# Scores of ten head pairs from float32r parts, sums of batch 0 by matmul, and an order made from other durations

## The chip, the cores and the metric

The kernel runs on one core of one Trainium2 chip. Its time is the device time of one execution in microseconds. It was executed three times; one further execution was profiled.

## What is computed

Softcapped attention over 4 batches, 12 heads, 448 positions and head size 64, then an MLP with squared ReLU; `cap` is 30.

```python
scores = scale * np.matmul(q, k.transpose(0, 1, 3, 2))
scores = cap * np.tanh(scores / cap)
scores = scores - np.max(scores, axis=-1, keepdims=True)
attn = np.exp(scores)
attn = attn / (np.sum(attn, axis=-1, keepdims=True) + 1e-09)
x = np.matmul(attn, v)              # heads side by side: 1792 x 768
h = x @ w_in                        # 768 x 2048
r = np.maximum(h, 0.0)
out = (r * r) @ w_out               # 2048 x 768
```

## The kernel before

Heads are taken in pairs, 24 of them, six to a batch, by `heads` (L187). A pair's scores come in four chunks of 112 keys. For a chunk, `qk` (L210) issues two float32 products of 64 rows, one for each head, in the two halves of the array, into a PSUM tile `s`; there are two such tiles. ScalarE (ACT) applies tanh (L224) and exp (L253). VectorE (DVE) adds the four chunks into `added` (L265). `pv` (L280) multiplies by `v` into `po`, with the heads side by side in columns. For the sums, `parts` (L346) transposes and reduces `added`, `whole_sum` (L353 to L360) makes reciprocals of it, `tr2` (L329) spreads them, `mult` (L334) scales, and `x_hi` and `x_lo` split the result in two float32r parts, `x`.

A branch at the start (L665) picks one of two programs by `cap`. With `cap` at most 40 the `bounded` one runs: no maximum is taken, and the sums go by DVE as said. The other has `ones` (L294), products with a tile of ones, and the steps `sums`, `tr1`, `rec` in the place of `parts` and `whole_sum`.

The weights come as 64-bit words that hold doubles. `convert` (L378) makes two float32r parts of each of 34 blocks, 16 of `w_in` and 18 of `w_out`, by `rebase` (L393, L395), `sign` and `low` (L405, L408), `whole` (L411), and the copies of L164/L166 and the differences of L169 into `w`. Batch 0 uses the blocks as they are converted; they are stored and loaded again for the other three batches. `unit` (L436) does the MLP: for each block and row tile three float32r products of 128 x 448, L455 to L457, into `f` (or `ff`); there are 2304 of them. ACT and DVE make `g` from it.

No loop over time stands in the code. Every piece of work is a `Step` with a key (a due time), a duration for each engine that may take it, and what it depends on. A planner at the end of `tile_body` (L544 to L638) takes the ready step of the lowest key for each engine, with these durations, buffer counts, and 0.15 us for PE when it goes over between whole products, products by rows (`qk`) and products by columns (`pv`). The order it finds is issued; each engine then runs its own list in order.

```python
            q = Step(T + (2 if b == 0 else QD) * c0, "PE", 0.75 * n_at, qk, [ready], new=s[cs] + t[cs], use=[raw], mode="rows")
```

Of the kernel before, what the change touches and what calls it, by code (L numbers as in the profile page):

```python
# [19 lines left out]
def tile_body(  # L20
# [11 lines left out]
    nc = tc.nc  # L32
# [10 lines left out]
    C0, LAT, TAIL = 4, 28, 30  # L43
    DMA, QSTEP, HOLD, PORT = 2.5, 2, 4, 15
    PVD, QD = 6, 2
    XH, GH, WH = 0.0, -2.0, 0.0
    ADD_FROM = 11
    PSTEP = [2, 2, 4, 4]
    W = [140, 145, 150, 120]
# [12 lines left out]
    def f(ap):  # L62
        return ap.bitcast(F32)
# [14 lines left out]
    for i in range(4):  # L78
        par = i % 2
        v32[par].append(const.tile([CP, NCH, 2 * D], F32, name=f"v32_{i}"))  # L80
        if not bounded:
            nc.vector.memset(v32[par][-1][:, :, D:2 * D] if par == 0 else v32[par][-1][:, :, 0:D], 1.0)
    nc.sync.dma_start(out=capb, in_=cap.to_broadcast([P, 1]))
    nc.vector.tensor_scalar_mul(capn, capb, -1.0)
    nc.vector.tensor_tensor(out=capa, in0=capb, in1=capn, op=ALU.max)
# [3 lines left out]
    if bounded:  # L89
        nc.scalar.activation(out=eps, in_=capa, func=AF.Exp, scale=-1.0)  # L90
        nc.vector.tensor_scalar_mul(eps, eps, 1e-9)
        added = [const.tile([P, 2, S], F32, name=f"added{i}") for i in range(2)]
        for a in added:
            nc.vector.memset(a[96:P], 0.0)
    else:
        nc.vector.memset(eps, 1e-9)

# [41 lines left out]
    steps = []  # L139

    class Step:
        def __init__(self, key, eng, dur, fn, deps=(), new=(), use=(), lag=0.15, behind=None, mode="full", port=False, calls=False):
            self.calls = calls
            self.key, self.fn, self.lag, self.mode = key, fn, lag, mode
            self.on, self.pen = dur if eng is None else ({eng: dur}, {eng: 0.0})
            self.any, self.taken, self.port = eng is None, False, port or eng is None
            self.new, self.use, self.after, self.wait = list(new), list(use) + list(new), [], 0
            for d in set(deps) | {u.maker for u in use}:
                d.after.append(self)
                self.wait += 1  # L150
# [19 lines left out]

    def COPY(n, act=0.0, dve=0.0):
        return (
            {"ACT": 0.1 + n * 0.00085, "DVE": 0.07 + n * 0.00055},
            {"ACT": act, "DVE": dve},
        )

    def EITHER(act, dve):
        return {"ACT": act, "DVE": dve}, {"ACT": 0.0, "DVE": 0.0}

    def SUB(n):  # L180
        return 0.07 + n * 0.00105
# [5 lines left out]
    def heads(p, T, n_at):  # L187
# [15 lines left out]

        ready = Step(T - 16, "SP", 1.5 * (p > 0), load, new=[raw], lag=3.0)
        got_v = Step(T, "SP", 1.4, load_v, new=vs, lag=3.0)

        tanhs = []
        for c0 in range(0, NCH, n_at):

            def qk(c0=c0):  # L210
                for c in range(c0, c0 + n_at):
                    ks = slice(c * CP, (c + 1) * CP)
                    for i in range(2):
                        r = slice(i * D, (i + 1) * D)
                        nc.tensor.matmul(  # L215
                            s[c].ap[0:CP, i, 0:S], raw.ap[r, 1, ks], raw.ap[r, 0], start=True, stop=True
                        )

            cs = slice(c0, c0 + n_at)
            q = Step(T + (2 if b == 0 else QD) * c0, "PE", 0.75 * n_at, qk, [ready], new=s[cs] + t[cs], use=[raw], mode="rows")  # L220
            for c in range(c0, c0 + n_at):

                def tanh(c=c):
                    nc.scalar.activation(out=t[c].ap, in_=s[c].ap[0:CP, :, 0:S], func=AF.Tanh, scale=c1[0:CP])  # L224

                tanhs.append(Step(T + 2 * c + 1, "ACT", 0.9, tanh, [q], use=[s[c], t[c]]))

        if not bounded:
            a = tanhs[0]
            for c in range(1, NCH):  # L230

                def top(c=c):
                    nc.vector.tensor_tensor(out=mx.ap, in0=t[0].ap if c == 1 else mx.ap, in1=t[c].ap, op=ALU.max)

                a = Step(
                    T + 2 * c + 3, "DVE", 1.01, top, [a, tanhs[c]], calls=c == NCH - 1,
                    new=[mx] * (c == 1), use=[t[c]] + ([t[0]] if c == 1 else [mx]), port=True,
                )
# [8 lines left out]
        for c in range(NCH):  # L247
# [6 lines left out]

            z = tanhs[c]
            if not bounded:
                z = Step(T + 14 + 2 * c, "DVE", 1.01, less, [a], use=[t[c], ma], port=True)
            exps.append(Step(T + EXP + 2 * c, "ACT", 0.95, exp, [z], use=[t[c]]))

        if n_add:  # L260
            ts = Buf("ts")
            for c in range(1, NCH):

                def add(c=c):
# [1 line left out]

                adds = [
                    Step(
                        T + EXP + 1 + 2 * c, "DVE", 1.01, add, exps[c - 1:c + 1] + adds,
                        new=[ts] * (c == 1), use=[t[c]] + ([t[0]] if c == 1 else [ts]), port=True,  # L270
                    )
                ]


        rows = [slice(0, D), slice(D, 2 * D)]

        by_ones = not bounded
# [16 lines left out]
        def ones(u, start, stop):  # L294
            for i in range(2):
                nc.tensor.matmul(
                    ss.ap[rows[i], 0:S], vs[i].ap[:, 0, rows[1 - i]], u.ap[:, i], start=start, stop=stop
                )

        n_pv = PSTEP[b]  # L300
# [50 lines left out]
        def whole_sum():  # L351
            r, o, z = (q.ap[:, i] for i in range(3))
            nc.vector.tensor_copy(o[0:64], r[64:128])  # L353
            nc.vector.tensor_tensor(out=z[0:64], in0=r[0:64], in1=o[0:64], op=ALU.add)
            nc.vector.tensor_copy(o[0:32], z[32:64])
            nc.vector.scalar_tensor_tensor(
                out=r[0:32], in0=z[0:32], scalar=eps[0:32], in1=o[0:32], op0=ALU.add, op1=ALU.add
            )
            for i in range(4):
                nc.vector.reciprocal(out=rc.ap[32 * i:32 * i + 32], in_=r[0:32, i // 2 * NB:(i // 2 + 1) * NB])  # L360

        T += NORM
        if by_ones:
            a = Step(T, None, EITHER(0.63, 0.56), sums, pvs[-1:], new=[sm], use=[ss])
            a = Step(T + 1, "DVE", 0.57, tr1, [a], new=[tr], use=[sm])
            a = Step(T + 1, "DVE", 0.17, rec, [a], new=[rc], use=[tr])
            a = Step(T + 1, "DVE", 0.56, tr2, [a], use=[rc, sm])
        else:
            a = Step(T, "DVE", 1.0, parts, adds, new=[q], use=[ts])
            a = Step(T, "DVE", 1.0, whole_sum, [a], new=[rc], use=[q])  # L370
            a = Step(T, "DVE", 0.64, tr2, [a], new=[sm], use=[rc])
        a = Step(T + 1, "DVE", 0.54, mult, [a] + pvs[-1:], new=[xf], use=[sm, po])
        a = Step(T + 2, None, COPY(448, dve=XH), x_hi, [a], new=[x], use=[xf])
        a = Step(T + 3, "DVE", SUB(448), x_lo, [a], use=[xf, x], port=True)
        x_t[b, h // 2], xdone[b, h // 2] = x, a
# [2 lines left out]
    def convert(T, src, dst, n):  # L378
# [44 lines left out]

        d = n / 6.0
        a = first = Step(T - 7, "SP", DMA * d, load, new=[raw], lag=4.0)
        m = Step(T, None, EITHER(0.91 * d, 0.83 * d), rebase, [a], new=[mag], use=[raw])
        a = Step(T, "DVE", 0.02 + 0.48 * d, sign, [a], new=[u], use=[raw], port=True)
        a = Step(T, "DVE", 0.02 + 0.48 * d, low, [a], use=[raw, u], port=True)
        a = Step(T, "DVE", 0.07 + 0.8 * d, whole, [a, m], use=[u, mag], port=True)
        a = Step(T, None, COPY(768 * d, dve=WH), w_hi, [a], new=[w], use=[u])  # L430
        a = Step(T, "DVE", SUB(768 * d), w_lo, [a], use=[u, w], port=True)
        loads[:] = [first]
# [32 lines left out]
    def up(T, d, b, m):  # L465
# [19 lines left out]
            sub(g.ap[:, 1], r.ap, f(g.ap)[:, 0])  # L485

        T += d
        a = Step(T, None, EITHER(0.54, 0.56), relu, done, new=[r], use=[hp])
        a = Step(T, "ACT", 0.53, square, [a], use=[r])
        a = Step(T, None, COPY(448, dve=GH), g_hi, [a], new=[g], use=[r])  # L490
        a = Step(T, "DVE", SUB(448), g_lo, [a], use=[r, g], port=True)
        g_t[b, m], gdone[b, m] = g, a
# [1 line left out]
    def down(T, d, b, dm, q, acc):  # L494
# [62 lines left out]
    while n_left:  # L557
        moved = False
        for e, q in ready.items():
# [15 lines left out]
            while q:  # L575
# [13 lines left out]
                if fit:  # L589
# [108 lines left out]
```

## Time and profile before

| what | value |
|---|---|
| median of 3 executions | 669.44 us (669.27 to 671.44) |
| profiled execution, its own time | 670.38 us |
| its span, first to last instruction | 668.6 us |
| PE busy | 646.4 us, 97% |
| DVE busy | 332.4 us, 50% |
| ACT busy | 333.5 us, 50% |
| granted clock of TensorE, mean | 0.989 |

The profiled execution took 1.8 us more than its span and 0.94 us more than the median. A busy PE is not a PE at its peak: matmuls are pipelined, and what one costs is the distance from its start to the next one's.

### The profile page before, as it was taken

Reading aid. Unit: us, or ns where it says so; the run is one execution under the profiler, and the core shown is the slowest. Engines: PE = TensorE matmul, PEld = TensorE weight load, DVE = VectorE, ACT = ScalarE, POOL = GpSimd, SP = SyncE. Lnnn points to the kernel's source line nnn. Section 1 sums busy time; section 2 is a strip of 40 time slices with the busy share of each in tenths; the row PEclk is TensorE's granted clock in tenths of the full one; section 3 lists DMA queues with packets and bytes.
Section 4 is the critical chain, followed back from the end, with each engine's and each line's share of the span. In section 5 each row is a group of like instructions: output and inputs, shape, how many; then the busy total and the mean of one; then the engine's idle time right before and its main releaser. Section 6 shows DMA issues by size and latency. Waiting matters only on the chain.

```text
span 668.6 us, 8034 instructions
## 1 busy us (share of the span) xinstructions
PE 646.4 (97%) x3072; PEld 486.2 (73%) x3072; DVE 332.4 (50%) x613; ACT 333.5 (50%) x456; POOL 0.2 (0%) x4
## 2 busy tenths in 40 slices
PE   4899998999999999999999999999999999999996
PEld 1234477667767798776798676767689999999996
DVE  3999999999999921565203146564620001110000
ACT  5899748677486425587202336858610005452000
POOL 0000000000000000000000000000000000000000
PEclk9799998999999999999999999999999999999999
DMA  8964587988899989864677576544348686666750
GB/s 204 301 181 131 154 264 269 331 283 273 297 311 333 336 286 335 236 181 137 191 239 235 182 235 184 166 156 140 97 156 262 223 280 227 222 187 205 257 162 31
DMA packets 57310, 148.46 MB, mean 222 GB/s; under 512 B 26288, under 2 KB 35504, under 8 KB 57264
## 3 DMA queue, kind: packets, MB, share of 16 engines
q1 hardware_dynamic: 57120, 147.64, 69.1%
q8 instruction: 26, 0.43, 0.3%
q10 hardware_dynamic: 144, 0.23, 0.1%
q14 instruction: 20, 0.16, 0.1%
HBM read 117.18 MB, written 30.67 MB: 221 GB/s over the span
## 4 chain that ended last, share of the span: by engine, by line
PE 88%; DVE 7%; DMA 2%; SPq 1%; issue 1%; ACT 1%; DVEq 0%
PE f L455 18%; PE f L457 17%; PE f L456 17%; PE s L215 10%; PE po L284 10%; PE ff L457 5%; PE ff L456 5%; PE ff L455 5%; DMA raw<-in_w_in_dram 2%; DVE added L265 1%; DVE u L411 1%; DVE w L169 1%; DVE rc L360 1%; DVE q L346 1%; DVE u L405 0%
## 5 line engine op out<-in xcount | busy, mean ns | idle before, releaser
L169 DVE TENSOR_TENSOR g<-r,g 128x448 fp32r<-128x448 f32 x64 | 39.6, 621 | 159.1 <-ACT g L164 158.9
L455 PE MATMUL f<-x,w 128*128 128x448 f32 x300 | 115.2, 384 | 3.0 <-DVE w L169 2.3
L457 PE MATMUL f<-x,w 128*128 128x448 f32 x300 | 110.5, 368 | 0.8 <-DVE x L169 0.7
L456 PE MATMUL f<-x,w 128*128 128x448 f32 x300 | 110.2, 367 | 0.0
L455 PE MATMUL f<-g,w 128*128 128x448 f32 x288 | 106.9, 371 | 0.5 <-DVE w L169 0.5
L457 PE MATMUL f<-g,w 128*128 128x448 f32 x288 | 105.2, 365 | 0.0
L456 PE MATMUL f<-g,w 128*128 128x448 f32 x288 | 105.2, 365 | 0.0
L224 ACT ACTIVATE t<-s,c 112x896 f32<-112x896 f32 x96 | 92.1, 1000 | 14.7 <-PE s L215 14.6
L253 ACT ACTIVATE t<-t,capa 112x896 f32<-112x896 f32 x96 | 96.3, 1039 | 0.2
L215 PE MATMUL s<-qkraw 64*112 64x448 f32 x368 | 83.6, 572 | 6.6 <-ACT t L224 6.6
L455 PEld LDWEIGHTS f<-x,w 128*128 128x128 f32 x300 | 56.7, 189 | 37.5 <-issue 24.4
L284 PE MATMUL po<-t,v 112*64 112x448 f32 x384 | 80.2, 561 | 0.0
L265 DVE TENSOR_TENSOR added<-added,t 112x896 f32<-112x896 f32 x48 | 52.1, 1085 | 48.7 <-ACT t L253 47.8
L455 PEld LDWEIGHTS f<-g,w 128*128 128x128 f32 x288 | 54.1, 188 | 14.5 <-issue 9.5
L457 PEld LDWEIGHTS f<-x,w 128*128 128x128 f32 x300 | 56.8, 189 | 6.4 <-DVE x L169 1.6
L505 ACT ACTIVATE o<-f 128x448 f32<-128x448 f32 x18 | 9.8, 545 | 102.8 <-PE f L457 102.8
L215 PEld LDWEIGHTS s<-qkraw 64*112 64x112 f32 x368 | 29.3, 174 | 43.2 <-issue 25.5
L456 PEld LDWEIGHTS f<-x,w 128*128 128x128 f32 x300 | 56.8, 189 | 3.9
L284 PEld LDWEIGHTS po<-t,v 112*64 112x64 f32 x384 | 26.1, 141 | 45.8 <-issue 42.1
L457 PEld LDWEIGHTS f<-g,w 128*128 128x128 f32 x288 | 54.1, 188 | 4.5
L456 PEld LDWEIGHTS f<-g,w 128*128 128x128 f32 x288 | 54.1, 188 | 4.2
L474 ACT ACTIVATE r<-f 128x448 f32<-128x448 f32 x42 | 22.7, 542 | 48.2 <-PE f L457 47.6
(52 smaller groups left out, 698.4 us busy)
## 6 DMA issues: line engine op xcount, KB each, us to landing
w<-k_in SPq DMA_DIRECT2D x48, 768.0 KB, 4.9
w<-k_out SPq DMA_DIRECT2D x36, 640.0 KB, 4.0
w<-k_out SPq DMA_DIRECT2D x18, 768.0 KB, 4.7
raw<-in_w_in_dram SPq DMA_DIRECT2D x16, 768.0 KB, 6.1
k_in<-w SPq DMA_DIRECT2D x16, 768.0 KB, 4.0
qkraw<-in_qkT_dram SPq DMA_DIRECT2D x46, 224.0 KB, 5.5
raw<-in_w_out_dram SPq DMA_DIRECT2D x12, 640.0 KB, 6.2
k_out<-w SPq DMA_DIRECT2D x12, 640.0 KB, 3.9
```

What stands on the lines that cost most here:

```text
L169: nc.vector.tensor_tensor(out=out, in0=in0, in1=in1, op=ALU.subtract)
L215: nc.tensor.matmul(s[c].ap[0:CP, i, 0:S], raw.ap[r, 1, ks], raw.ap[r, 0], start=True, stop=True)
L224: nc.scalar.activation(out=t[c].ap, in_=s[c].ap[0:CP, :, 0:S], func=AF.Tanh, scale=c1[0:CP])
L253: nc.scalar.activation(out=t[c].ap, in_=t[c].ap, func=AF.Exp, scale=capa[0:CP])
L265: nc.vector.tensor_tensor(out=ts.ap[0:CP], in0=t[0].ap if c == 1 else ts.ap[0:CP], in1=t[c].ap, op=ALU.add)
L284: nc.tensor.matmul(po.ap[rows[i], 0:S], vs[i].ap[:, c, rows[i]], t[c].ap[:, i], start=c == 0, stop=c == NCH - 1)
L346: nc.vector.tensor_reduce(out=q.ap[:, 0], in_=ts.ap.rearrange("p i (j c) -> p (i j) c", c=32), axis=mybir.AxisListType.X, op=ALU.add, appl ...
L455: nc.tensor.matmul(o, w.ap[:, 1, j], x[:, 0], start=first and j == 0, stop=False)
L456: nc.tensor.matmul(o, w.ap[:, 0, j], x[:, 0], start=False, stop=False)
L457: nc.tensor.matmul(o, w.ap[:, 0, j], x[:, 1], start=False, stop=last and j == n - 1)
L474: nc.scalar.activation(out=r.ap, in_=hp.ap[:, 0:S], func=AF.Relu)
L505: nc.scalar.activation(out=o.ap, in_=acc.ap[:, 0:S], func=AF.Copy)
```

## The change

It does five things.

- Pairs 14 to 23 (`SPLIT = 14`) get operands `m` and `lo`. For each head the high float32r part of q and k is copied into one half of the partitions of `m`; k's high part goes again into the other half, beside q's low part; k's low part goes into `lo`. That is two copies of 64 x 896, two of 64 x 448 and four differences of 64 x 448 a pair. A block of two chunks is then four products of 128 rows (k high with q high and q low) and four of 64 rows (k low with q high), one float32r pass each, in the place of four float32 products of 64 rows.
- In pairs 0 to 5 (`ONES = 6`) the sums go by `ones` on `added` and by `sums`, `tr1`, `rec`, in the place of `parts` and `whole_sum`.
- In the other pairs `whole_sum` takes the reciprocals in two instructions rather than four, with one more copy.
- `added` and the tiles of ones are set by GpSimd (POOL); before, DVE set `added`, and the bounded program set no ones.
- The planner's durations are other numbers, and with them the order of nearly every step.

```diff
+    SPLIT, SPT, ONES = B * H, -6.0, B * H
...
+        SPLIT, ONES = 14, 6
...
-        if not bounded:
-            nc.vector.memset(v32[par][-1][:, :, D:2 * D] if par == 0 else v32[par][-1][:, :, 0:D], 1.0)
+        nc.gpsimd.memset(v32[par][-1][:, :, D:2 * D] if par == 0 else v32[par][-1][:, :, 0:D], 1.0)
...
-            nc.vector.memset(a[96:P], 0.0)
+            nc.gpsimd.memset(a[96:P], 0.0)
...
+                def hi(eng, i=i, r=r):
+                    copy(eng, m[i].ap[r], raw.ap[r])
+                def k_hi(eng, i=i, r=r, o=o):
+                    copy(eng, m[i].ap[o, 1], raw.ap[r, 1])
+                def q_lo(i=i, r=r, o=o):
+                    sub(m[i].ap[o, 0], raw.ap[r, 0], f(m[i].ap)[r, 0])
+                def k_lo(i=i, r=r):
+                    sub(lo.ap[r], raw.ap[r, 1], f(m[i].ap)[r, 1])
...
+                for c in range(c0, c0 + n_at) if split else ():
+                        nc.tensor.matmul(
+                            s[c].ap[0:CP, i, 0:S], m[i].ap[:, 1, ks], m[i].ap[:, 0], start=True, stop=False
+                        )
+                for c in range(c0, c0 + n_at) if split else ():
+                        nc.tensor.matmul(
+                            s[c].ap[0:CP, i, 0:S], lo.ap[rows[i], ks], m[i].ap[rows[i], 0], start=False, stop=True
+                        )
...
-        by_ones = not bounded
+        by_ones = p < ONES
...
-            for i in range(4):
-                nc.vector.reciprocal(out=rc.ap[32 * i:32 * i + 32], in_=r[0:32, i // 2 * NB:(i // 2 + 1) * NB])
+            for i in range(2):
+                nc.vector.reciprocal(out=rc.ap[rows[i]], in_=r[0:64, i * NB:(i + 1) * NB])
...
-        a = Step(T, "DVE", 0.02 + 0.48 * d, sign, [a], new=[u], use=[raw], port=True)
+        a = Step(T, "DVE", 0.155 + 0.45 * d, sign, [a], new=[u], use=[raw], port=True)
```

Three places of the order. First PE at the first block of scores of pair 14 (`s` scores, `f` the MLP's sums), before and after:

```order
L457 MATMUL f<-x,w 128x448
L215 MATMUL s<-qkraw 112x448 x4
L455 MATMUL f<-x,w 128x448
L456 MATMUL f<-x,w 128x448
L457 MATMUL f<-x,w 128x448
```

```order
L497 MATMUL f<-x,w 128x448
L243 MATMUL s<-m 112x448 x4
L249 MATMUL s<-m,lo 112x448 x4
L495 MATMUL f<-x,w 128x448
L496 MATMUL f<-x,w 128x448
L497 MATMUL f<-x,w 128x448
```

The block stands between MLP products in both; one group of four products has become two groups of four.

Second, DVE in the first conversions and the sums of pair 0 (`u` and `w` belong to the weights, `q`, `rc`, `tr`, `sm` and `xf` to the sums), before and after:

```order
L346 TENSOR_REDUCE q<-added_141 128x28
L408 TENSOR_SCALAR u<-raw 128x768
L353 COPY q<-q 64x28
L354 TENSOR_TENSOR q<-q 64x28
L355 COPY q<-q 32x28
L356 SCALAR_TENSOR_TENSOR q<-q,eps 32x28
L360 RECIPROCAL rc<-q 32x14 x4
L411 SCALAR_TENSOR_TENSOR u<-mag,u 128x768
L329 STREAM_TRANSPOSE sm<-rc 128x448
L265 TENSOR_TENSOR added_142<-t 112x896
L334 TENSOR_TENSOR xf<-po,sm 128x448
```

```order
L362 STREAM_TRANSPOSE tr<-sm 128x448
L445 TENSOR_SCALAR u<-raw 128x768
L365 RECIPROCAL rc<-tr 128x14
L448 TENSOR_SCALAR u<-raw 128x768
L368 STREAM_TRANSPOSE sm<-rc 128x448
L451 SCALAR_TENSOR_TENSOR u<-mag,u 128x768
L373 TENSOR_TENSOR xf<-po,sm 128x448
```

Nine instructions of the sums before `sm` have become a transpose and one reciprocal; between them stand steps of the next weight block.

Third, PE after the change at the sums of pair 0 (`po` of L335 takes the sums, `added` has been made by DVE):

```order
L323 MATMUL po<-t,v_0_130 64x448
L323 MATMUL po<-t,v_1_132 64x448
L335 MATMUL po<-added_145,v_0_130 64x448
L335 MATMUL po<-added_145,v_1_132 64x448
L256 MATMUL s<-qkraw 112x448 x10
```

The two products of L335 are new; ten products of scores stand behind them.

## Rows read from the trace of the kernel before

**Rows 1.** The page: busy time, granted clock in 40 slices, shares of the chain.

```profile
PE 646.4 (97%) x3072; PEld 486.2 (73%) x3072; DVE 332.4 (50%) x613; ACT 333.5 (50%) x456; POOL 0.2 (0%) x4
...
PEclk9799998999999999999999999999999999999999
...
PE 88%; DVE 7%; DMA 2%; SPq 1%; issue 1%; ACT 1%; DVEq 0%
```

**Rows 2.** Stretches (us): length, busy of each engine (instructions), clock, DMA share, GB/s.

```profile
40.00:60.00 20.00, 19.98 (x97) 8.04 (x94) 19.46 (x40) 19.46 (x23) 0.00 (x0) 1.00 0.56 171
...
100.00:150.00 50.00, 47.67 (x221) 34.52 (x220) 48.97 (x83) 38.50 (x56) 0.00 (x0) 0.97 0.85 295
...
300.00:350.00 50.00, 50.00 (x245) 39.74 (x244) 14.12 (x25) 16.97 (x25) 0.00 (x0) 1.00 0.60 185
...
400.00:450.00 50.00, 50.00 (x240) 33.41 (x241) 28.35 (x54) 35.83 (x49) 0.00 (x0) 1.00 0.54 166
```

**Rows 3.** Waits of PE: total us, times, longest us.

```profile
PE s L215 <- ACT t L224: 7.5, 5, 2.3
...
PE f L455 <- DVE w L169: 2.8, 2, 2.3
PE f L457 <- DVE x L169: 0.7, 1, 0.7
```

**Rows 4.** The chain of waits near 103 us: start us, us, what.

```profile
102.49 0.88 DVE w L169
...
103.41 0.47 PE f L455
```

**Rows 5.** PE in order of time around one block of scores: start us, us, instruction.

```profile
375.66 0.36 PE L456 MATMUL f<-g,w 128*128 128x448 f32 x1
375.86 0.37 PE L457 MATMUL f<-g,w 128*128 128x448 f32 x1
376.16 1.76 PE L215 MATMUL s<-qkraw 64*112 64x448 f32 x8
377.85 0.47 PE L455 MATMUL f<-g,w 128*128 128x448 f32 x1
378.16 0.37 PE L456 MATMUL f<-g,w 128*128 128x448 f32 x1
```

**Rows 6.** Weight loads of `pv` in order of time, inside one block.

```profile
371.41 0.14 PEld L284 LDWEIGHTS po<-t,v 112*64 112x64 f32 x2 [0.23 <-issue]
371.78 0.14 PEld L284 LDWEIGHTS po<-t,v 112*64 112x64 f32 x2 [0.23 <-issue]
```

**Rows 7.** Groups of DVE by line and shape: busy us, mean ns, idle before.

```profile
L346 DVE TRANSPOSE_TENSOR_REDUCE q<-added 128x28 f32<-128x896 f32 x24 | 26.6, 1107 | 0.4
...
L360 DVE RECIPROCAL rc<-q 32x14 f32<-32x14 f32 x96 | 22.2, 231 | 2.7
...
L329 DVE STREAM_TRANSPOSE sm<-rc 128x448 f32<-128x448 f32 x24 | 15.3, 639 | 0.2
...
L356 DVE SCALAR_TENSOR_TENSOR q<-q,eps 32x28 f32<-32x28 f32 x24 | 5.6, 235 | 0.8
...
L476 DVE TENSOR_SCALAR r<-f 128x448 f32<-128x448 f32 x8 | 5.0, 623 | 12.0 <-PE f L457 12.0
L395 DVE TENSOR_SCALAR mag<-raw 128x768 f32<-128x768 f32 x8 | 4.4, 550 | 0.0
L166 DVE CAST w<-u 128x768 fp32r<-128x768 f32 x8 | 4.4, 548 | 0.2
L354 DVE TENSOR_TENSOR q<-q 64x28 f32<-64x28 f32 x24 | 4.3, 180 | 0.8
L353 DVE COPY q<-q 64x28 f32<-64x28 f32 x24 | 4.2, 176 | 0.8
```

**Rows 8.** DVE in order of time, first 13 us.

```profile
2.68 1.75 DVE L94 MEMSET added<- 32x896 f32 x2 [2.68 <-issue]
...
12.12 1.09 DVE L265 TENSOR_TENSOR added<-t 112x896 f32<-112x896 f32 x1 [3.50 <-ACT t L253]
```

More of the change, by code (lines that the diff above doesn't have):

```diff
@@ L45, in tile_body @@
     PVD, QD = 6, 2
-    XH, GH, WH = 0.0, -2.0, 0.0
+    SPLIT, SPT, ONES = B * H, -6.0, B * H
+    XH, GH, WH, EH = 0.0, -2.0, 0.0, 0.0
     ADD_FROM = 11
@@ L112, in tile_body @@
         "o": ("hlf", [P, S], F32, 2, 0), "u": ("blk", None, U32, 2, 4), "mag": ("blk", None, F32, 2, 4),
+        "m": ("blk", [P, 2, S], F32R, 4, 2), "lo": ("hlf", [P, S], F32R, 2, 1),
         "first": ("free", None, None, 1, 0), "v0": ("free", None, None, 2, 0), "v1": ("free", None, None, 2, 0),
@@ L141, in tile_body, with __init__ @@
     class Step:
-        def __init__(self, key, eng, dur, fn, deps=(), new=(), use=(), lag=0.15, behind=None, mode="full", port=False, calls=False):
-            self.calls = calls
+        def __init__(self, key, eng, dur, fn, deps=(), new=(), use=(), lag=0.15, behind=None, mode="full", port=False, calls=False, turn=0.19):
+            self.calls, self.turn = calls, turn
             self.key, self.fn, self.lag, self.mode = key, fn, lag, mode
@@ L172, in COPY @@
         return (
-            {"ACT": 0.1 + n * 0.00085, "DVE": 0.07 + n * 0.00055},
+            {"ACT": 0.21 + n * 0.00082, "DVE": 0.155 + n * 0.00051},
             {"ACT": act, "DVE": dve},
@@ L177, in EITHER @@
     def EITHER(act, dve):
-        return {"ACT": act, "DVE": dve}, {"ACT": 0.0, "DVE": 0.0}
+        return {"ACT": act, "DVE": dve}, {"ACT": 0.0, "DVE": EH}
     def SUB(n):
-        return 0.07 + n * 0.00105
+        return 0.155 + n * 0.00104
     x_t, g_t, xdone, gdone, loads = {}, {}, {}, {}, []
@@ L205, in heads @@
         got_v = Step(T, "SP", 1.4, load_v, new=vs, lag=3.0)
+        rows = [slice(0, D), slice(D, 2 * D)]
+        split = p >= SPLIT
+        operands, used = [ready], [raw]
+        if split:
+            m, lo = [Buf("m"), Buf("m")], Buf("lo")
+            used = m + [lo]
+            for i in range(2):
+                r, o = rows[i], rows[1 - i]
+                def hi(eng, i=i, r=r):
[6 more added lines that the diff above has]
+                    sub(lo.ap[r], raw.ap[r, 1], f(m[i].ap)[r, 1])
+                a = Step(T + SPT, None, COPY(896), hi, [ready], new=[m[i]] + [lo] * (i == 0), use=[raw])
+                operands += [
+                    Step(T + SPT + 1, None, COPY(448), k_hi, [ready, a], use=[raw, m[i]]),
+                    Step(T + SPT + 1, "DVE", 0.62, q_lo, [a], use=[raw, m[i]], port=True),
+                    Step(T + SPT + 1, "DVE", 0.62, k_lo, [a], use=[raw, m[i], lo], port=True),
+                ]
         tanhs = []
@@ L210, in qk @@
             def qk(c0=c0):
-                for c in range(c0, c0 + n_at):
+                for c in range(c0, c0 + n_at) if split else ():
+                    ks = slice(c * CP, (c + 1) * CP)
+                    for i in range(2):
+                        nc.tensor.matmul(
+                            s[c].ap[0:CP, i, 0:S], m[i].ap[:, 1, ks], m[i].ap[:, 0], start=True, stop=False
+                        )
+                for c in range(c0, c0 + n_at) if split else ():
+                    ks = slice(c * CP, (c + 1) * CP)
+                    for i in range(2):
+                        nc.tensor.matmul(
+                            s[c].ap[0:CP, i, 0:S], lo.ap[rows[i], ks], m[i].ap[rows[i], 0], start=False, stop=True
+                        )
+                for c in () if split else range(c0, c0 + n_at):
                     ks = slice(c * CP, (c + 1) * CP)
@@ L219, in heads @@
             cs = slice(c0, c0 + n_at)
-            q = Step(T + (2 if b == 0 else QD) * c0, "PE", 0.75 * n_at, qk, [ready], new=s[cs] + t[cs], use=[raw], mode="rows")
+            q = Step(T + (2 if b == 0 else QD) * c0, "PE", (0.595 if split else 0.75) * n_at, qk, operands, new=s[cs] + t[cs], use=used, mode="rows", turn=0.0 if split else 0.19)
             for c in range(c0, c0 + n_at):
@@ L224, in tanh @@
                     nc.scalar.activation(out=t[c].ap, in_=s[c].ap[0:CP, :, 0:S], func=AF.Tanh, scale=c1[0:CP])
-                tanhs.append(Step(T + 2 * c + 1, "ACT", 0.9, tanh, [q], use=[s[c], t[c]]))
+                tanhs.append(Step(T + 2 * c + 1, "ACT", 1.0, tanh, [q], use=[s[c], t[c]]))
         if not bounded:
@@ L235, in heads @@
                 a = Step(
-                    T + 2 * c + 3, "DVE", 1.01, top, [a, tanhs[c]], calls=c == NCH - 1,
+                    T + 2 * c + 3, "DVE", 1.085, top, [a, tanhs[c]], calls=c == NCH - 1,
                     new=[mx] * (c == 1), use=[t[c]] + ([t[0]] if c == 1 else [mx]), port=True,
@@ L256, in heads @@
             if not bounded:
-                z = Step(T + 14 + 2 * c, "DVE", 1.01, less, [a], use=[t[c], ma], port=True)
-            exps.append(Step(T + EXP + 2 * c, "ACT", 0.95, exp, [z], use=[t[c]]))
+                z = Step(T + 14 + 2 * c, "DVE", 1.085, less, [a], use=[t[c], ma], port=True)
+            exps.append(Step(T + EXP + 2 * c, "ACT", 1.04, exp, [z], use=[t[c]]))
         if n_add:
@@ L268, in heads @@
                     Step(
-                        T + EXP + 1 + 2 * c, "DVE", 1.01, add, exps[c - 1:c + 1] + adds,
+                        T + EXP + 1 + 2 * c, "DVE", 1.085, add, exps[c - 1:c + 1] + adds,
                         new=[ts] * (c == 1), use=[t[c]] + ([t[0]] if c == 1 else [ts]), port=True,
@@ L272, in heads @@
                 ]
-        rows = [slice(0, D), slice(D, 2 * D)]
-        by_ones = not bounded
+        by_ones = p < ONES
         acc = [po, ss] if by_ones else [po]
@@ L296, in ones @@
                 nc.tensor.matmul(
-                    ss.ap[rows[i], 0:S], vs[i].ap[:, 0, rows[1 - i]], u.ap[:, i], start=start, stop=stop
+                    ss.ap[rows[i], 0:S], vs[i].ap[:, 0, rows[1 - i]], u.ap[0:CP, i], start=start, stop=stop
                 )
@@ L355, in whole_sum @@
             nc.vector.tensor_copy(o[0:32], z[32:64])
+            nc.vector.tensor_copy(o[32:64], z[0:32])
             nc.vector.scalar_tensor_tensor(
-                out=r[0:32], in0=z[0:32], scalar=eps[0:32], in1=o[0:32], op0=ALU.add, op1=ALU.add
+                out=r[0:64], in0=z[0:64], scalar=eps[0:64], in1=o[0:64], op0=ALU.add, op1=ALU.add
             )
-            for i in range(4):
-                nc.vector.reciprocal(out=rc.ap[32 * i:32 * i + 32], in_=r[0:32, i // 2 * NB:(i // 2 + 1) * NB])
+            for i in range(2):
+                nc.vector.reciprocal(out=rc.ap[rows[i]], in_=r[0:64, i * NB:(i + 1) * NB])
         T += NORM
         if by_ones:
[L364 to L367, printed above, removed]
-        else:
-            a = Step(T, "DVE", 1.0, parts, adds, new=[q], use=[ts])
-            a = Step(T, "DVE", 1.0, whole_sum, [a], new=[rc], use=[q])
+            a = Step(T, None, EITHER(0.64, 0.68), sums, pvs[-1:], new=[sm], use=[ss])
+            a = Step(T + 1, "DVE", 0.64, tr1, [a], new=[tr], use=[sm])
+            a = Step(T + 1, "DVE", 0.24, rec, [a], new=[rc], use=[tr])
+            a = Step(T + 1, "DVE", 0.64, tr2, [a], use=[rc, sm])
+        else:
+            a = Step(T, "DVE", 1.11, parts, adds, new=[q], use=[ts])
+            a = Step(T, "DVE", 1.4, whole_sum, [a], new=[rc], use=[q])
             a = Step(T, "DVE", 0.64, tr2, [a], new=[sm], use=[rc])
-        a = Step(T + 1, "DVE", 0.54, mult, [a] + pvs[-1:], new=[xf], use=[sm, po])
+        a = Step(T + 1, "DVE", 0.62, mult, [a] + pvs[-1:], new=[xf], use=[sm, po])
         a = Step(T + 2, None, COPY(448, dve=XH), x_hi, [a], new=[x], use=[xf])
@@ L425, in convert @@
         a = first = Step(T - 7, "SP", DMA * d, load, new=[raw], lag=4.0)
-        m = Step(T, None, EITHER(0.91 * d, 0.83 * d), rebase, [a], new=[mag], use=[raw])
-        a = Step(T, "DVE", 0.02 + 0.48 * d, sign, [a], new=[u], use=[raw], port=True)
-        a = Step(T, "DVE", 0.02 + 0.48 * d, low, [a], use=[raw, u], port=True)
-        a = Step(T, "DVE", 0.07 + 0.8 * d, whole, [a, m], use=[u, mag], port=True)
+        m = Step(T, None, EITHER(0.18 + 0.73 * d, 0.155 + 0.4 * d), rebase, [a], new=[mag], use=[raw])
+        a = Step(T, "DVE", 0.155 + 0.45 * d, sign, [a], new=[u], use=[raw], port=True)
+        a = Step(T, "DVE", 0.155 + 0.45 * d, low, [a], use=[raw, u], port=True)
+        a = Step(T, "DVE", 0.155 + 0.8 * d, whole, [a, m], use=[u, mag], port=True)
         a = Step(T, None, COPY(768 * d, dve=WH), w_hi, [a], new=[w], use=[u])
@@ L487, in up @@
         T += d
-        a = Step(T, None, EITHER(0.54, 0.56), relu, done, new=[r], use=[hp])
-        a = Step(T, "ACT", 0.53, square, [a], use=[r])
+        a = Step(T, None, EITHER(0.545, 0.62), relu, done, new=[r], use=[hp])
+        a = Step(T, "ACT", 0.576, square, [a], use=[r])
         a = Step(T, None, COPY(448, dve=GH), g_hi, [a], new=[g], use=[r])
@@ L508, in store @@
             nc.sync.dma_start(out=outT[dm * P:(dm + 1) * P, b * S:(b + 1) * S], in_=o.ap)
-        a = Step(T + d, "ACT", 0.46, evac, done, new=[o], use=[acc])
+        a = Step(T + d, "ACT", 0.545, evac, done, new=[o], use=[acc])
         Step(T + d, "SP", 0.7, store, [a], use=[o], lag=3.0)
@@ L598, in tile_body @@
                     if e == "PE" and st.mode != mode:
-                        dur += 0.15
+                        dur += st.turn if st.mode != "full" else 0.19
                         mode = st.mode
```

## The prediction

> **What bounds the kernel now.** I read the page first: PE is busy for 97% of the span and makes 88% of the chain that ended last; DVE makes 7% [rows 1]. So the time is PE's own list of work plus what PE loses while it waits. Then the stretches: in 40 to 60 us DVE and ACT are both busy for 19.46 of 20 us, and PE still for 19.98; in 300 to 350 us PE is full while DVE has 14.12 of 50 and ACT 16.97 [rows 2]. Work taken off PE after some 250 us should therefore come off the time whole; in the first 180 us it counts only as far as DVE and ACT keep up. The waits of PE say where they don't: 7.5 us for tanh, 2.8 us for weight blocks, 0.7 us for `x` [rows 3]. The chain shows the largest of the second kind: DVE ends a weight block at 103.37, and PE starts on it at 103.41 [rows 4]. In the stretch around it the clock stands at 0.97, the mean of 1.2 and 2.4 GHz [rows 2], so after that idle time 0.03 x 50 = 1.5 us more was lost.
>
> **Scores of ten pairs.** A pair has two blocks of two chunks, so 20 blocks change. The old price is read from one block among MLP products. An MLP product costs 375.86 - 375.66 = 0.20 us. From the last product ahead of the block to the second one behind it there are 378.16 - 375.86 = 2.30 us, in which two steps are those of MLP products: the block costs 2.30 - 0.406 = 1.894 us, at 0.203 a product [rows 5]. Eight records in pairs are four steps; a step of float32 pairs is seen bare in `pv`, 371.78 - 371.41 = 0.37, some 0.375 us [rows 6]. Four of them are 1.50, so going into the row form and out of it costs 0.39 us a block.
>
> The new block is four products of 128 rows, 4 x 0.203 = 0.81, and two pairs of 64 rows, one pass each, 2 x 0.19 (half of 0.375) = 0.38. Without any price for the change of form that is 1.19, say 1.20 us; with the whole 0.39 it is 1.59. No row shows the change of form between two float32r products: every one that the trace has lies next to float32 products. I take 1.50, three quarters of the way to the end that the rows show, since it is paid at every block there. The gain is 20 x (1.894 - 1.50) = 7.9 us, between 6.1 (1.59) and 13.9 (1.20).
>
> The Trainium skill, page TensorEngine Tiling (Array Packing), Tiling Modes, says that a change of the tiling mode drains the engine. By that rule the four products of L249 pay going in and out whatever their type; the block is 1.59 us and the gain 6.1. Rows 5 agree so far as they go: 0.39 us a block, with float32.
>
> The operands are made off PE. Two copies of 896 elements at no more than the 1.09 us of an addition of that size [rows 8], and six instructions of 448 at no more than 0.623 us [rows 7], are 5.9 us a pair, 59 us in all, shared by DVE and ACT between some 260 and 480 us. There DVE stands at 14 to 28 of 50 us and ACT at 17 to 36 [rows 2], so I cost it at nothing. Were they late, PE's whole list would stand behind L243.
>
> **Sums of batch 0.** PE gains two float32 products a pair, which are four records or two steps of a `pv` block: 2 x 0.375 = 0.75 us [rows 6], 6 x 0.75 = 4.5 us. The columns' form is there already. I count all of it; the least is nothing, if it falls into the 7.5 us in which PE waits for tanh [rows 3].
>
> DVE loses, for each of the six pairs, 1.107 + 0.176 + 0.180 + 0.235 + 4 x 0.231 = 2.62 us (with the smallest copy left out), and gains a transpose, 0.639, and a reciprocal, some 0.231: 1.75 us less a pair, 10.5 us for six [rows 7]. By the order this lies ahead of the eighth weight block, which is the one PE waited for. Ahead of it DVE also takes over two `mag` at 0.550, two copies of `w` at 0.548 and one `sums` at some 0.623, 2.8 us in all [rows 7]. So that block comes 10.5 - 2.8 = 7.7 us earlier, against a wait of 2.3, and PE has the same 37 units (111 MLP products) ahead of it in both orders. The wait goes, the one of 0.5 later and the 0.7 for `x` with it, and the 1.5 us of clock: 2.8 + 0.7 + 1.5 = 5.0 us, between 0 and, with some of the waits for tanh, 7. Next in line is ACT, which gets five `sums` of at most 0.62 us and hands over the two `mag` and two copies: about even, so the tanh waits stay.
>
> **The rest.** `whole_sum` with two reciprocals less and one copy more, 2 x 0.231 - 0.176 = 0.29 us on DVE in 18 pairs, lies under PE. POOL's six memsets have to write 4 x 256 + 2 x 896 = 2816 elements a partition; DVE took 1.75 us for 1792 of them. Even at three times that rate's price, 8.3 us from 2.68 on, they end at 11, before the first addition at 12.12 [rows 8]. Nothing.
>
> **The sum.** -7.9 + 4.5 - 5.0 = -8.4 us on the profiled execution's 670.38, which is 662.0; the median stood 0.94 lower, so **661.0 us**.
>
> **Rivals** (all against the median).
> - *The whole price of the form.* Drained at both ends, 1.59 us a block: -6.1 + 4.5 - 5.0 = -6.6, 662.8 us. For it: rows 5 show it at every block. Chance 0.2.
> - *No price for the form.* The 0.39 us belongs to float32 products and their doubled loads, not to the half arrays: 1.20 us, -13.9 + 4.5 - 5.0 = -14.4, 655.0 us. Against it: going in and out of `pv`, another form, is paid too. Chance 0.2.
> - *PE's waits stay.* DVE is ahead, but ACT was as full as DVE in 40 to 60 us [rows 2], and a chain through PE, ACT and DVE takes the place of one on DVE alone. What PE no longer waits for in `w` it waits for in `x`: -7.9 + 4.5 = -3.4, 666.0 us. Chance 0.2; of it I give a quarter to no change.
> - *The half arrays don't overlap.* If the two 64-row float32r products run one after the other, the block is 8 x 0.203 + 0.39 = 2.01, 20 x 0.12 = 2.3 us more than before: +2.3 + 4.5 - 5.0 = +1.8, 671.2 us, no change to speak of. Against it: the float32 pairs overlap in rows 5. Then the change would not do what it says. Chance 0.05.
> - *Slower: the products with ones hold up PE.* They wait for the third addition of their pair on DVE, where before nothing on PE did, and the scores that feed ACT are queued behind them. DVE is full in 40 to 60 us [rows 2]. If each of the six waits 2.5 us, 15 us are added: -7.9 + 4.5 - 5.0 + 15 = +6.6, 676.0 us. It decides against the change from (8.4 + 2) / 6 = 1.7 us a wait. Against it: DVE has just become 1.75 us a pair lighter, and the additions stand early in its list. Chance 0.08.
>
> **How the numbers follow.** The forecast keeps 0.27. A measurement of this kernel tells about 0.3%, 2 us, from no change. Faster: 0.27 + 0.2 + 0.2 + 0.15 = 0.82; within 0.3%: 0.05 + 0.05 = 0.10; slower 0.08. The range goes from 654, just under the case without a price, to 667.5, over the case with the waits. It leaves out the last two rivals, 0.13, and a little below.
>
> **What would show it.** After the change, blocks of L243 and L249 should cost some 1.50 us between MLP products, by the same reading as in rows 5; 1.2 or 1.6 decide between the first rivals, and 2.0 would mean no overlap. The wait of `f` for DVE `w` should be gone, and the clock at 1.00 in 100 to 150 us. A wait of PE at L335 for `added`, or at L243 for `m`, would make the prediction wrong, the more so with the clock falling behind it. PE's busy time should fall by about 3 us, and its waits after 60 us to under 1 us.

## The result, and the profile after

The changed kernel takes 660.38 us (median of 4, 659.98 to 661.03) against 669.67 us for the kernel before: ratio 0.9857, 95% interval 0.9837 to 0.9877, 9.3 us faster. The profiled execution took 660.59 us; its span is 658.7 us, 9.9 less than before. The forecast was 661.0.

The page of the changed kernel, the same lines as in [rows 1]:

```profile
PE 640.5 (97%) x3096; PEld 493.3 (75%) x3096; DVE 356.3 (54%) x629; ACT 338.9 (51%) x464; POOL 2.9 (0%) x10
...
PEclk9899999999999999999999999999999999999999
...
PE 95%; ACT 2%; DMA 1%; SPq 1%; DVE 0%; issue 0%
```

DVE has left the chain, 7% to 0%, though its busy time rose by 24 us. PE's busy time fell by 5.9 us, twice the 3 us that the prediction named as a sign. The waits of PE in the changed kernel (total us, times, longest us), all that there are:

```profile
PE s L256 <- ACT t L265: 8.1, 5, 3.3
PE s L256 <- DMA first<-in_qkT_dram: 5.2, 1, 5.2
```

The waits for `w` and `x` of [rows 3] are gone; the one for tanh has stayed. The stretches of the changed kernel, columns as in [rows 2]:

```profile
40.00:60.00 20.00, 19.90 (x97) 8.34 (x95) 18.02 (x29) 18.80 (x23) 0.00 (x0) 1.00 0.73 211
...
100.00:150.00 50.00, 50.00 (x242) 37.23 (x241) 45.87 (x83) 38.48 (x57) 0.00 (x0) 1.00 0.91 313
...
300.00:350.00 50.00, 50.00 (x248) 39.66 (x246) 21.06 (x41) 18.45 (x26) 0.00 (x0) 1.00 0.64 193
...
400.00:450.00 50.00, 50.00 (x247) 36.98 (x246) 39.92 (x76) 34.90 (x48) 0.00 (x0) 1.00 0.44 145
```

In 40 to 60 us DVE has fallen from 19.46 to 18.02, in 100 to 150 us PE is full and the clock at 2.4 GHz throughout. The new operands stand in the last row, 39.92 us of DVE in place of 28.35, and PE does not notice. One new block of scores in order of time, to be read as [rows 5]:

```profile
262.34 0.36 PE L496 MATMUL f<-x,w 128*128 128x448 f32 x1
262.54 0.36 PE L497 MATMUL f<-x,w 128*128 128x448 f32 x1
262.74 0.97 PE L243 MATMUL s<-m 128*112 128x448 f32 x4
263.64 0.67 PE L249 MATMUL s<-m,lo 64*112 64x448 f32 x4
264.24 0.47 PE L495 MATMUL f<-x,w 128*128 128x448 f32 x1
264.55 0.36 PE L496 MATMUL f<-x,w 128*128 128x448 f32 x1
```

264.55 - 262.54 - 0.406 = 1.604 us. Over the 20 blocks the median of this reading is 1.603 us, and over the 35 old blocks of the kernel before that stand between MLP products 1.887. The four products of 128 rows go on at 0.20 us each; the first of 64 rows comes only 0.90 us after the first of them.

**A ledger for PE.** From the trace's starts I add up PE's list of work at these prices (0.202 us an MLP or whole product, 0.375 a step of a float32 pair, 0.19 of a float32r pair, 0.195 for each change of form) and call the rest, up to the start of an MLP product, lost. It covers idle time, the lower clock and the first 5 us.

| lost (us) before MLP product | 1st | 37th | 112th | 601st | last |
|---|---|---|---|---|---|
| kernel before | 20.2 | 22.3 | 25.2 | 28.1 | 28.8 |
| changed kernel | 19.8 | 20.0 | 20.2 | 20.2 | 21.2 |

PE's list went from 634.2 to 632.3 us, 1.9 less; what it lost fell by 7.6. The sum, 9.5, stands beside 9.9 of the span. Four fifths of the gain is time that PE had lost, all of it in the first 250 us. Some 1.8 us of the 7.6 is lower clock in the first 40 us: its means over 20 us each were 0.89 and 0.85 before, 0.96 and 0.87 after, so 5.2 and 3.4 us were lost to it. That the change brings this is not shown: executions of the kernel before differ by as much among themselves (mean clock 0.988 to 0.994).

### The profile page after: what moved, and what is told of

Read it like the earlier page. It is cut to its first block, busy times and chain, and to the rows that moved or that the text cites. A ratio compares the mean times of both kernels' runs of the same rounds, so it can differ in the third digit from the quotient of the medians.

```text
span 658.7 us, 8106 instructions
## 1 busy us (share of the span) xinstructions
PE 640.5 (97%) x3096; PEld 493.3 (75%) x3096; DVE 356.3 (54%) x629; ACT 338.9 (51%) x464; POOL 2.9 (0%) x10
## 4 chain that ended last, share of the span: by engine, by line
PE 95%; ACT 2%; DMA 1%; SPq 1%; DVE 0%; issue 0%
PE f L495 20%; PE f L496 18%; PE f L497 18%; PE po L323 12%; PE s L256 6%; PE ff L496 6%; PE ff L495 6%; PE ff L497 6%; PE s L243 2%; PE s L249 2%; DMA raw<-in_w_in_dram 1%; ACT t L265 1%; PE po L335 1%; ACT t L294 1%; SPq L704 0%; SPq L200 0%
## 5 line engine op out<-in xcount | busy, mean ns | idle before, releaser
L256 PE MATMUL s<-qkraw 64*112 64x448 f32 x208 | 47.1, 569 | 7.2 <-ACT t L265 7.1
L519 ACT ACTIVATE r<-r 128x448 f32<-128x448 f32 x64 | 36.5, 574 | 5.7 <-DVE r L516 4.4
```

What stands on the lines that cost most here:

```text
L256: nc.tensor.matmul(s[c].ap[0:CP, i, 0:S], raw.ap[r, 1, ks], raw.ap[r, 0], start=True, stop=True)
L519: nc.scalar.activation(out=r.ap, in_=r.ap, func=AF.Square)
```

## The experiments

Beside each group of experiments the kernel before ran again on the same chip (669.8 to 670.1 us); ratios are against it. The first two sections take the change apart: the scores, the sums, and the planner's durations, on or off.

### The change without one or both of its parts

`no_ones`:

```diff
-        SPLIT, ONES = 14, 6
+        SPLIT, ONES = 14, 0
```

> Pairs 0 to 5 take their sums by DVE again; all else as in the change, the durations too. PE loses 12 pairs of float32 products, 4.5 us. Theory A (what PE lost to waiting came back because the products with ones make DVE lighter): the waits for weight blocks and the lower clock return, 5 to 7.6 us, so 661 to 663.5 us. Theory B (it came back because the order was made from better durations): they stay away, 660.4 - 4.5 = 655.9 us.

Measured: 662.91 us, ratio 0.9894 (0.9876 to 0.9913).

`no_split`:

```diff
-        SPLIT, ONES = 14, 6
+        SPLIT, ONES = B * H, 6
```

> The scores of all pairs are float32 products of 64 rows again; the rest as in the change. By the trace a new block costs 1.60 us against 1.89, 0.29 x 20 = 5.8 us: 666.2 us by both theories. If the predicted 1.50 were right, 7.9: 668.3 us. If late operands cost PE something that the trace doesn't show, less than 666.

Measured: 666.02 us, 0.9927 (0.9903 to 0.9950).

`neither`:

```diff
-        SPLIT, ONES = 14, 6
+        SPLIT, ONES = B * H, 0
```

> No float32r scores and no products with ones; what is left is the order from the new durations, the memsets on POOL and the shorter reciprocals. Theory A: the waits are back as in no_ones and the scores cost 5.8 us more, 667 to 669.5 us. Theory B: 660.4 - 4.5 + 5.8 = 661.7 us.

Measured: 663.54 us, 0.9899 (0.9881 to 0.9917).

`no_split` is 5.6 us over the changed kernel: the 20 blocks at 1.887 - 1.603 us, 5.7, whole. The time of `no_ones` lies in the range of theory A. Its waits of PE:

```profile
PE s L256 <- ACT t L265: 6.4, 7, 2.4
PE s L256 <- DMA first<-in_qkT_dram: 5.0, 1, 5.0
PE f L495 <- DVE w L171: 2.8, 2, 2.5
PE f L497 <- DVE x L171: 0.8, 1, 0.8
PE f L495 <- ACT x L166: 0.5, 1, 0.5
```

The largest of those for `w` in order of time (start us, us, instruction), and the clock in the stretch after it:

```profile
223.74 0.83 DVE L171 TENSOR_TENSOR w<-u,w 128x640 fp32r<-128x640 f32 x1
224.62 0.47 PE L495 MATMUL f<-g,w 128*128 128x448 f32 x1 [2.48 <-DVE w L171]
```

```profile
225.00:250.00 25.00, 24.93 (x116) 21.39 (x115) 12.92 (x21) 11.52 (x17) 0.00 (x0) 0.93 0.95 342
```

A wait of 2.5 us for a weight block, now until 224.62 us, and 25 x 0.07 = 1.75 us of clock behind it. But `neither` fits neither theory: without the products with ones it stands 6 us under the kernel before, and these are its waits for `w` and `x`:

```profile
PE f L495 <- ACT x L166: 1.1, 1, 1.1
PE f L497 <- DVE x L171: 1.0, 1, 1.0
PE f L495 <- DVE w L171: 0.4, 1, 0.4
```

So most of the lost time can be had back without them. It also means that leaving the products with ones out does not alone bring the wait of `no_ones`. Both kernels have the same order on PE, ACT and DVE up to 212 us. There `no_ones` puts the first copies for pair 14 on ACT, and PE takes MLP products where `neither` has scores. `neither` has no such wait. With both parts of the change there is none either, so here it takes the new scores and the missing products with ones together; which of the moved steps makes it is not shown.

### The same under the durations of before

`old_dur`, the planner's durations set back for every step that both kernels have:

```diff
-            {"ACT": 0.21 + n * 0.00082, "DVE": 0.155 + n * 0.00051},
+            {"ACT": 0.1 + n * 0.00085, "DVE": 0.07 + n * 0.00055},
...
-        return 0.155 + n * 0.00104
+        return 0.07 + n * 0.00105
...
```

> Both parts of the change, but the planner's durations of the steps that both kernels have are those of the kernel before (also for the sums, and 0.15 us for a change of form). Theory A: 660 to 661.5 us, and PE waits after 60 us for less than 1.5 us. Theory B: the waits are those of before, 5 to 7.6 us, 665.5 to 668 us.

Measured: 659.34 us, 0.9844 (0.9828 to 0.9860).

`old_ones`, on these durations, and `old_split`:

```diff
-        SPLIT, ONES = 14, 6
+        SPLIT, ONES = B * H, 6
```

> Durations of the kernel before, scores as before, pairs 0 to 5 with products with ones: that part of the change alone. Theory A (the products with ones take back PE's waits by making DVE lighter, whatever the order): +4.5 us of PE's list, -7.6 of waits, 669.7 - 3.1 = 666.6 us, no wait of f for DVE w. Theory C (it takes the two parts together): the waits stay and 4.5 us are added, 674 us.

Measured: 665.60 us, 0.9936 (0.9918 to 0.9953). PE's waits for `w` and `x` are gone.

```diff
-        SPLIT, ONES = 14, 6
+        SPLIT, ONES = 14, 0
```

> Durations of the kernel before, sums as before, ten pairs with float32r scores: that part alone. Theory A: 20 blocks at 0.29 us less and the waits of before, 669.7 - 5.8 = 663.9 us, with the wait of f for DVE w of 2 to 3 us. Theory D (moving the order by any small thing is enough to lose the waits): 656 to 660 us.

Measured: 661.15 us, 0.9867 (0.9843 to 0.9891), with 1.9 us of waits for `w`.

The new durations aren't what made the change faster: with both parts the old ones do as well, 659.3 against 660.4. `old_ones` agrees with theory A to 1 us, but it has the shorter reciprocals and the memsets too. `old_split` is 2.8 us under the 663.9 that its blocks explain, so something smaller in the change had to be tried by itself.

### The two small things alone

`old_neither` is the kernel before with POOL's memsets and the shorter reciprocals. PE and ACT have exactly the order of before; so has DVE outside `whole_sum` and the memsets. The edit, as it stands against the kernel before:

```diff
...
-            for i in range(4):
-                nc.vector.reciprocal(out=rc.ap[32 * i:32 * i + 32], in_=r[0:32, i // 2 * NB:(i // 2 + 1) * NB])
+            for i in range(2):
+                nc.vector.reciprocal(out=rc.ap[rows[i]], in_=r[0:64, i * NB:(i + 1) * NB])
```

> Durations, scores and sums of the kernel before; of the change only the memsets on POOL and the two reciprocals in the place of four are left. PE's order is that of the kernel before. If these two small things are worth nothing, 669.7 us and a wait of f for DVE w of some 2.8 us. old_split stood 2.8 us under what its blocks alone explain; if the lighter sums on DVE (0.29 us a pair) did that, 667 us here and a shorter wait.

Measured: 665.89 us, 0.9937 (0.9921 to 0.9953): 4.2 us of the gain, from what the prediction had put at nothing. DVE in order of time in one `whole_sum`, the kernel before and then `old_neither`:

```profile
87.83 0.18 DVE L353 COPY q<-q 64x28 f32<-64x28 f32 x1
...
88.73 1.02 DVE L360 RECIPROCAL rc<-q 32x14 f32<-32x14 f32 x4
89.78 0.61 DVE L408 TENSOR_SCALAR u<-raw 128x768 uint16<-128x768 uint16 x1
```

```profile
94.78 0.17 DVE L392 COPY q<-q 64x28 f32<-64x28 f32 x1
...
95.86 0.50 DVE L400 RECIPROCAL rc<-q 64x14 f32<-64x14 f32 x2
96.39 0.96 DVE L451 SCALAR_TENSOR_TENSOR u<-mag,u 128x768 uint32<-128x768 uint32 x1
```

From its first copy to the next step it takes 1.61 us in place of 1.95. Eight of these stand ahead of the eighth weight block, in a stretch in which DVE has no other rest: 2.7 us. `old_split` has the same order up to some 250 us and so is a second trace of it. DVE at the second block of raw weights and at the end of the eighth converted one, in the kernel before, `old_split` and `old_neither`:

```profile
20.16 0.61 DVE L405 TENSOR_SCALAR u<-raw 128x768 uint16<-128x768 uint16 x1 [1.22 <-DMA raw<-in_w_in_dram]
102.41 0.95 DVE L169 TENSOR_TENSOR w<-u,w 128x768 fp32r<-128x768 f32 x1
```

```profile
20.69 0.61 DVE L445 TENSOR_SCALAR u<-raw 128x768 uint16<-128x768 uint16 x1 [1.26 <-DMA raw<-in_w_in_dram]
100.40 0.95 DVE L171 TENSOR_TENSOR w<-u,w 128x768 fp32r<-128x768 f32 x1
```

```profile
18.49 0.61 DVE L445 TENSOR_SCALAR u<-raw 128x768 uint16<-128x768 uint16 x1
98.28 0.95 DVE L171 TENSOR_TENSOR w<-u,w 128x768 fp32r<-128x768 f32 x1
```

From the start of the one to the end of the other it is 83.20, 80.66 and 80.74 us: 2.5 us less in both. In the profiled execution of `old_neither` the block is ready 4.1 us earlier; the other 1.7 come from before the first shortened sum, where the raw weights had landed and DVE did not wait for them. This execution took 664.03 us, 1.9 less than its kernel's median. The wait of PE for the block did not go, since PE comes to it earlier too. What `old_neither` has left of waits for `w`, and the clock in 100 to 150 us:

```profile
PE f L495 <- DVE w L171: 1.7, 2, 1.5
```

```profile
100.00:150.00 50.00, 50.00 (x241) 36.05 (x239) 49.30 (x87) 40.93 (x59) 0.00 (x0) 1.00 0.92 317
```

So the 4.2 us are, as an estimate from these rows, 2.5 us of DVE, by which everything behind it comes earlier, and the 1.5 us of clock that PE no longer loses after the wait.

The memsets were not tried apart from the reciprocals; they set free 1.75 us of DVE before 4.5 us [rows 8], when it was waiting for `cap` anyway, in the kernel before until here:

```profile
6.50 0.15 DVE L84 TENSOR_SCALAR capn<-capb 128x1 f32<-128x1 f32 x1 [2.08 <-DMA capb<-in_cap_dram]
```

The ledger of these kernels:

| lost (us) before MLP product | 1st | 37th | 112th | 601st | last |
|---|---|---|---|---|---|
| old_neither | 19.0 | 18.8 | 21.1 | 22.2 | 22.8 |
| old_ones | 17.4 | 18.6 | 18.9 | 18.9 | 19.2 |
| old_split | 20.4 | 20.9 | 23.2 | 24.3 | 26.0 |
| no_ones | 13.8 | 21.1 | 21.1 | 26.0 | 27.8 |

Reading down from `old_neither` to `old_ones`: the products with ones save 3.6 us more of the lost time and put 4.9 on PE's list (six times two steps of 0.375, and two changes of form more). That makes 1.3 us more, and the two profiled executions differ by 1.5 (664.03 and 665.55); the medians are the same, 665.9 and 665.6.

All eight combinations (medians, us), each with the shorter reciprocals and the memsets:

| | neither part | ones | new scores | both |
|---|---|---|---|---|
| new durations | 663.54 | 666.02 | 662.91 | 660.38 |
| durations of before | 665.89 | 665.60 | 661.15 | 659.34 |

The products with ones cost 2.5 us or bring 2.5 beside the new durations, without and with the new scores; beside the old durations they bring 0.3 and 1.8. Steps of 2 us are at the edge of the noise, as each time has an interval of 1.1 to 1.6 us on either side. The new scores bring 5.6, 4.7 and 6.3 us, near the 5.7 of their blocks, but only 0.6 from `neither` to `no_ones`, where the wait until 224.62 us and the clock behind it, 4.2 us, take most of the rest. The parts don't add: each moves the planner's order.

### What the form of a block costs

`no_lo` leaves out the products of k's low part with q's high part, so the scores lack that term:

```diff
-                            s[c].ap[0:CP, i, 0:S], m[i].ap[:, 1, ks], m[i].ap[:, 0], start=True, stop=False
-                        )
-                for c in range(c0, c0 + n_at) if split else ():
...
-                            s[c].ap[0:CP, i, 0:S], lo.ap[rows[i], ks], m[i].ap[rows[i], 0], start=False, stop=True
+                            s[c].ap[0:CP, i, 0:S], m[i].ap[:, 1, ks], m[i].ap[:, 0], start=True, stop=True
```

> The change without its 80 products of 64 rows (k low with q high), so part of the scores is left out; order and operands as they are. If the 0.39 us for the change of form is paid by these products alone, a block is 4 x 0.203 = 0.81 us, and 20 x 0.79 = 15.8 us go: 644.6 us. If a block of scores pays it whatever its form, only their stream goes, 20 x 0.38 = 7.6: 652.8 us.

Measured: 645.17 us, 15.2 under the changed kernel. PE at one of its blocks:

```profile
260.94 0.36 PE L491 MATMUL f<-x,w 128*128 128x448 f32 x1
261.14 0.97 PE L243 MATMUL s<-m 128*112 128x448 f32 x4
261.95 0.36 PE L489 MATMUL f<-x,w 128*128 128x448 f32 x1
```

The block costs 261.95 - 260.94 - 0.203 = 0.81 us. So the products of 64 rows cost 0.79 us a block for 0.38 of stream: the other 0.4 is the way into the half arrays and back, and float32r pays it as float32 did.

`rows14` makes all three products of 64 rows, from one copy and one difference of 128 x 896 a pair:

```diff
...
+                parts = ((m, m), (m, lo), (lo, m)) if split else ()
+                for j, (kp, qp) in enumerate(parts):
+                    for c in range(c0, c0 + n_at):
...
+                            nc.tensor.matmul(
+                                s[c].ap[0:CP, i, 0:S], kp.ap[rows[i], 1, ks], qp.ap[rows[i], 0], start=j == 0, stop=j == 2
+                            )
...
```

> The change with blocks of rows alone in the ten pairs: all three float32r products (high by high, high by low, low by high) of 64 rows, heads side by side, from one copy and one difference of 128 x 896 a pair. A block is six steps of 0.19 and the change of form, 0.39: 1.53 us against 1.60, 20 x 0.07 = 1.4 us less: 659.0 us. If 64-row products cost as much as whole ones, 6 x 0.203 + 0.39 = 1.61, no difference.

Measured: 658.40 us, 0.9840 (0.9820 to 0.9859). PE around a block:

```profile
260.54 0.37 PE L481 MATMUL f<-x,w 128*128 128x448 f32 x1
260.84 0.66 PE L233 MATMUL s<-m 64*112 64x448 f32 x4
261.34 0.57 PE L233 MATMUL s<-lo,m 64*112 64x448 f32 x4
261.75 0.57 PE L233 MATMUL s<-m,lo 64*112 64x448 f32 x4
262.25 0.47 PE L479 MATMUL f<-x,w 128*128 128x448 f32 x1
262.55 0.37 PE L480 MATMUL f<-x,w 128*128 128x448 f32 x1
```

262.55 - 260.54 - 0.406 = 1.604: the block has the same price, as pairs go on at 0.20 us and not at 0.19. The 2 us by which it beats the changed kernel therefore don't come from its blocks, and the two intervals overlap; whether it is faster is not settled. In its profiled execution the clock stood at 1.00 in the first 40 us, where the changed kernel lost 3.4 us to it; its two executions at the changed kernel's mean clock, 0.993, took 660.1 and 660.9 us, no less than the changed kernel. It does need less of DVE, 328.9 us busy against 356.3; ACT is as busy, 339.6 against 338.9.

### How many pairs

`ones3`:

```diff
-        SPLIT, ONES = 14, 6
+        SPLIT, ONES = 14, 3
```

> Products with ones in pairs 0 to 2 alone, otherwise the change. PE's list is 2.25 us shorter. If three pairs make DVE light enough, 658.1 us and no wait for w; if not, the waits of no_ones come back in part, 661 us or more.

Measured: 660.81 us, 0.9866 (0.9841 to 0.9892), and 2.0 us of waits for `w`: as fast as with six, the shorter list being given back in waits.

`rows10a` and `rows6b` take the blocks of `rows14` to earlier pairs. The limits that the planner keeps for `m` and `lo` had to be changed with it; only the first line of the edit is shown:

```diff
-        SPLIT, ONES = 14, 6
+        SPLIT, ONES = 10, 6
```

> As rows14, from pair 10 on (limits on m and lo tightened so that the planner finds an order): eight blocks more at 0.36 us, 656.1 us. If the operands of pairs 10 to 13 come late, PE waits at its scores and the gain is less.

Measured: 665.59 us, 0.9926 (0.9908 to 0.9945), with 4.8 us of waits for `w` and 0.6 for `lo`.

```diff
-        SPLIT, ONES = 14, 6
+        SPLIT, ONES = 6, 6
```

> As rows14, from pair 6 on: 36 blocks. 1.4 + 16 x 0.36 = 7.2 us under the change, 653.2 us, if DVE, 46 to 47 of 50 us busy in 100 to 200 us, takes 12 us more there without PE waiting. If not, a wait of f for DVE w or of scores for lo comes up and the time stays over 656 us.

Measured: 665.90 us, 0.9940 (0.9919 to 0.9961). The waits of PE in `rows6b`:

```profile
PE f L479 <- DVE w L171: 5.6, 3, 2.8
PE s L240 <- ACT t L249: 5.5, 5, 2.1
...
PE f L481 <- DVE x L171: 0.9, 1, 0.9
PE s L233 <- ACT t L249: 0.8, 2, 0.4
```

In these two kernels, shorter blocks where DVE still converts weights cost more in waits than they save: PE's list in `rows6b` is 6 to 7 us shorter than in the changed kernel, and it loses 31.5 us in place of 21.2. How much of that is owed to the limits was not tried. That the change begins at pair 14 seems to belong to its gain.

## Why the prediction was right, and where not

The time was right to 0.6 us; three terms of the sum were not, and that they made up for each other is luck.

- **Scores, -7.9 forecast, -5.7 measured.** The mechanism held; the price of the block was mis-sized. I took 1.50 us, below the row's 1.59, and it is 1.603. The rival with the whole price of the form was right: `no_lo` shows that the price goes with the 64-row products, 0.4 us a block, in float32r as in float32. The Trainium skill, TensorEngine Tiling (Array Packing), Tiling Modes, says that changing the tiling mode drains TensorE. The trace agrees so far as each visit to the half arrays has this price; that it is a drain, no run here shows.
- **The operands at nothing.** Right in the change: PE waits neither at L243 nor at L249, and `no_split` gives back just what the blocks are worth. `no_ones` shows that it isn't so in every order: there the new scores come with a wait for `w` that takes most of what they bring, be it by the operands or by the products drawn forward.
- **Sums, +4.5.** Right as PE's list goes (4.9 with the changes of form, `old_neither` to `old_ones`). No wait at L335 appeared, so the slower rival fell.
- **PE's waits, -5.0 forecast, -7.6 measured.** The rows named were the right ones, and all went, and with them a wait of 0.6 us for `x` from ACT; some 1.8 us is the clock of the first 40 us. The margin was too large: the eighth block, until 103.36 us before, was to come 7.7 us earlier and comes 3.6 earlier, at 99.78, as DVE has another order and now waits for others itself, here 0.78 us for ACT:

```profile
98.82 0.96 DVE L171 TENSOR_TENSOR w<-u,w 128x768 fp32r<-128x768 f32 x1 [0.78 <-ACT w L166]
```

- **The rest, "under PE. Nothing".** This step failed. The shorter reciprocals and the memsets alone are worth 4.2 us. I had read DVE as full in 40 to 60 us and as what PE waited for at 103 us, and counted 1.75 us a pair there for the sums, but put 0.29 us a pair of the same engine in the same stretch under PE. That PE's lost time came back is therefore not owed to the products with ones alone, as I had argued: two reciprocals fewer bring back the clock and 2.5 us of DVE. The wait at the eighth block falls to 1.5 us with them and goes with the products with ones, but these then pay with PE's own time, and what they brought beside the reciprocals went either way in the table. The memsets were right at nothing as far as the traces go: POOL was busy for 2.9 us in all.
- **ACT next in line, tanh waits stay.** Right: 7.5 us before, 8.1 after.

## What to carry to other kernels

A cost may be put under another engine only stretch by stretch: the same 0.3 us on DVE meets no wait of PE at 400 us and, eight times over, is worth 2.5 us and a clock loss at 100 us. Before paying with the bounding engine's time for relief of another, try the relief that costs nothing, here fewer instructions for the same reciprocals. A step between forms of the array is paid for each visit, 0.4 us with four products in half arrays as with twelve, so it is counted by visits, not by products. Where a planner makes the order anew, a part's worth read from one pair of kernels may not hold in another.

## What the runs showed that was not expected

- A float32r product of 64 rows is no cheaper per step than a whole one: pairs go on at 0.20 us (`rows14`), so a block of twelve in half arrays costs what the mixed block does, 1.60 us.
- A reciprocal of 64 x 14 takes 234 ns, one of 32 x 14 231 ns [rows 7]; the row in the changed kernel (busy us, mean ns, idle before):

```profile
L400 DVE RECIPROCAL rc<-q 64x14 f32<-64x14 f32 x36 | 8.4, 234 | 1.1
```

- Three waits of PE for a weight block, of 2.3 to 2.5 us, were followed by 1.5 to 1.75 us of lower clock (the kernel before at 103 us, `no_ones` at 225, `rows10a` at 157), so their price was some 1.7 times their length. A longer one was not: in `rows6b` PE waited 2.8 us until 227.27 us, and the clock stayed up.

```profile
227.27 0.47 PE L479 MATMUL f<-g,w 128*128 128x448 f32 x1 [2.82 <-DVE w L171]
```

```profile
225.00:250.00 25.00, 22.73 (x120) 19.91 (x121) 10.42 (x17) 12.06 (x18) 0.00 (x0) 1.00 0.83 304
```
